# A packed-attention and feed-forward kernel: one table orders all engines up to the first rest, three quarters of one batch come first, and its second softmax has the tokens on the partitions

## The chip, the cores and the metric

The kernel runs on one core of one Trainium2 chip. The metric is the device time of one execution in microseconds. A core has the matrix engine TensorE (PE in the profile, PEld for its weight loads), VectorE (DVE), ScalarE (ACT), GpSimd (POOL) and SyncE (SP, which here only issues DMA transfers). Each works through its own queue in order and waits for the others by semaphores. SBUF is the working memory, PSUM (8 banks) takes what PE writes.

## The reference

`q`, `k`, `v` are [8, 8, 576, 64] (batch, head, token, width) and `p` is [8, 8, 32, 64], 32 "packs" for each head.

```python
def sm_attn(qq, kk, vv):
    s = scale * np.matmul(qq, kk.transpose(0, 1, 3, 2))
    s = s - np.max(s, axis=-1, keepdims=True)
    a = np.exp(s)
    a = a / (np.sum(a, axis=-1, keepdims=True) + 1e-09)
    return np.matmul(a, vv)
p_packed = sm_attn(p, k, v)                 # softmax over 576 tokens
out = sm_attn(q, p_packed, p_packed)        # softmax over 32 packs
x = out.transpose(0, 2, 1, 3).reshape(B * S, H * D)   # 4608 x 512
h = x @ w_in                                # 512 x 2048
return (h * sigmoid(h)) @ w_out             # 2048 x 512
```

## The kernel before

**Batches and units.** The feed-forward part never forms `out`. For each batch the packed result is multiplied into w_in (`packs_in`, a quarter of the 2048 columns at a time), and the second softmax's shares are the moving side of the hidden product. A unit (b, f) is 128 of the 2048 hidden columns of one batch. Its hidden product `h_unit` (L535) has 12 matmuls of 288 tokens, 6 for each half of the tokens, with upper and lower parts (`a_hi`, `a_lo`, `pw_hi`, `pw_lo`) for precision. ScalarE then makes `g` and `g_hi` (L538, L539), VectorE `g_lo` (L541), and the output product `out_unit` (L549) has 12 matmuls of 512 that add into PSUM over all f. Of the 288 tokens of a half, 256 go this way; the last 32 are collected in `rest` and come as four rest units for two batches.

**Attention of a batch.** First scores (L223, packs against keys), their maxima, an exponential, the exponentials turned so that tokens lie on the partitions, the packed product with `v` (L300), scaling, a turning of the result (L319), second scores (L223, packs against `q`). Then VectorE turns the second scores in 32x32 blocks (L336) so that each group of 32 packs lies along a row, takes maxima, subtracts (L339, L340), ScalarE exponentiates (L343), VectorE sums, divides and turns back (L346 to L353), and `a_hi` and `a_lo` are split (L357, L358).

**Weights.** `w_in` and `w_out` come as 64-bit numbers, 16 chunks of 1 MB, two in each quarter and matrix. Each is scaled by ScalarE (L172, L173), joined by VectorE (L178, L179, L181, and L182 for w_in; for w_out GpSimd adds, L182), and w_out is split (L190, L191).

**Order before.** Up to the mark where `manual_schedule` begins, a scheduler that plans with its own model of time puts the instructions in order, within pins (`PINS`, `WARM`, `STEPS`). The 32 early units run in `BLOCKS`, pairs (batch, quarter): two batches are interleaved, and each is added up in two parts (`parts` in DRAM). `keep_warm` (L107) multiplies the identity by itself. From the first rest on, the order is the program's, and batches 2 to 7 follow one another.

Of the kernel before, what the change touches and what calls it, by code (L numbers as in the profile page):

```python
# [19 lines left out]
P = 128  # L20
# [8 lines left out]
NJ = 4  # L29
# [8 lines left out]
BLOCKS = [(0, 0), (0, 1), (1, 0), (1, 1), (1, 2), (0, 2), (0, 3), (1, 3)]  # L38

WARM = (16, 2), (7, 4), (3, 2), (4, 2), (3, 2)  # L40
WARM_END = 10

PINS = (
    ("", "nm"),
    (("tT", 1), ("less", 0)),
    (("exp", 0), ("a2T", 0)),
    (("exp", 0), ("a2", 0)),
)

# [16 lines left out]
def packed_attention_ffn(ctx: ExitStack, tc: tile.TileContext, pkT, qT, vA, vB, w_in, w_out, out):  # L66

# [20 lines left out]
    ps_h = ent(tc.tile_pool(name="ps_h", bufs=1, space=PSUM))  # L88
    ps_s = ent(tc.tile_pool(name="ps_s", bufs=1, space=PSUM))
# [3 lines left out]
    win = const.tile([P, NJ, NI, JW], I32, name="win")  # L93
# [8 lines left out]
    def keep_warm(times):  # L102

        ps = ps_h.tile([P, 2, 512], F32, name="ps_hid")
        with after("pe"):
            for _ in range(times):
                made["pe"] = nc.tensor.matmul(ps[:, 0, :P], ident, ident, start=True, stop=True)  # L107

    def after(name):
        return tc.issue_after(made[name].ins) if name in made else nullcontext()  # L110

    def load_pk(b):
# [4 lines left out]
        return t[:, :P], t[:, P : P + NI * S].rearrange("p (hf i s) -> p hf i s", hf=2, i=NI)  # L117

    def load_q(b):
        t = kvq.tile([P, 5 * DM], F32, name="kvq_t")  # L120
        n = NI * HS
        for c in (slice(0, n), slice(n, 2 * n)) if b == 0 else (slice(0, 2 * n),):
            made["q_load", b] = nc.sync.dma_start(t[:, c], qT[b, :, c])
            if b == 0 and c.start == 0:
                weights.fetch(1)
        return t[:, : NI * S].rearrange("p (hf i s) -> p hf i s", hf=2, i=NI)

    def load_v(b):
        t = kvq.tile([P, 5 * DM], F32, name="kvq_t")
        nc.sync.dma_start(t[:, : 4 * DM], vA[b])  # L130
        nc.sync.dma_start(t[: S - 4 * P, 4 * DM :], vB[b])
        return t.rearrange("p (c e) -> p c e", c=5)

    class Weights:
# [5 lines left out]
        chunks = [(j, i, inner) for j in range(NJ) for inner in (True, False) for i in (0, 2)]  # L140

        def __init__(self, stage):
            self.stage, self.raw, self.n, self.fetched = stage, {}, 0, 0

            rings = [["stage", "stage", NJ - 2, NJ - 1], ["stage", "stage", NJ - 1], ["stage", "stage"]]
            self.place, self.after = [], []
            for n in range(len(self.chunks)):
                first = (0, 8, 12)[(n >= 8) + (n >= 12)]
                ring = rings[(n >= 8) + (n >= 12)]
                place = ring[(n - first) % len(ring)]  # L150
                before = [m for m in range(n) if self.place[m] == place]
                self.after.append((before[-2:-1] if place == "stage" else before[-1:]) or [-3])
                self.place.append(place)

        def fetch(self, ready):

            n = self.fetched
            if n == len(self.chunks) or self.after[n][0] > ready:
                return False
            self.fetched += 1  # L160
            if self.place[n] == "stage":
                raw = self.stage.tile([P, 4 * JW], I32, name="w_raw")
            else:
                raw = win[:, self.place[n]].rearrange("p i n -> p (i n)")
            j, i, inner = self.chunks[n]
            made["fetch", n] = nc.sync.dma_start(raw.bitcast(I64), (w_in if inner else w_out)[:, j, i // 2])
            self.raw[n] = raw.rearrange("p (n two) -> p two n", two=2)
            return True

        def scale(self, n):  # L170
            low, up = self.raw[n][:, 0], self.raw[n][:, 1].bitcast(F32)
            nc.scalar.activation(low, low.bitcast(U32), AF.Copy, scale=2.0**-29)  # L172
            nc.scalar.activation(up, up, AF.Copy, scale=2.0**-112)  # L173

        def join(self, n):
            j, i, inner = self.chunks[n]
            low, up = self.raw[n][:, 0], self.raw[n][:, 1]
            nc.vector.tensor_scalar(up.bitcast(F32), up.bitcast(F32), TOP, -TOP, op0=ALU.min, op1=ALU.max)  # L178
            nc.vector.scalar_tensor_tensor(low, up, -(2**31), low, op0=ALU.bitwise_and, op1=ALU.bitwise_or)  # L179
            z = win[:, j, i : i + 2].rearrange("p i n -> p (i n)") if inner else up  # L180
# [3 lines left out]
        def split(self, n):  # L184
            j, i, inner = self.chunks[n]
            w = self.raw.pop(n)[:, 1].bitcast(F32)
            if not inner:
                f = FJ * j + i
                hi, lo = (t[:, f : f + 2].rearrange("p i n -> p (i n)") for t in (wo_hi, wo_lo))
                nc.scalar.copy(hi, w)  # L190
                nc.vector.tensor_tensor(lo, w, hi.bitcast(F32), ALU.subtract)  # L191

        def step(self):

            n, last = self.n, len(self.chunks)
            self.n += 1
            while self.fetch(n - 2):
                pass
            if n < last:
                self.scale(n)  # L200
            if n - 1 in self.raw:
                self.join(n - 1)
                self.split(n - 1)

    def side_banks(b):

        if b:
            return ps_s.tile([P, 2, 512], F32, name="ps_side")
        return ps_acc.tile([P, 2, 512], F32, name="ps_acc")

    turns = [ps_h, ps_s]

    def two_banks():

        turns.reverse()
        return turns[0].tile([P, 2, 512], F32, name="ps_hid" if turns[0] is ps_h else "ps_side")

    def heads(bank, lhs, rhs, n):

        for par in range(2):  # L220
            r = slice(D * par, D * par + D)
            for i in range(NI):
                made["pe"] = nc.tensor.matmul(  # L223
                    bank(par)[NP * i : NP * i + NP, :n], lhs(r, i), rhs(r, i), start=True, stop=True
                )
# [4 lines left out]
    def attention(b):  # L230

        (p, k), v = made.pop(("kv", b))
        ps = [side_banks(b) for _ in range(2)] if b == 0 else []
        s1 = None if b == 0 else scratch(S).rearrange("p (r s) -> p r s", r=2)
        for hf in range(2):
# [496 lines left out]
```

## Time and profile before

| | us |
|---|---|
| three runs, median (lowest, highest) | 743.69 (743.69, 744.9) |
| profiled execution, time | 743.93 |
| profiled execution, span of its instructions | 742.1 |

Rows of a group read: line, engine, operation, output <- input, shapes, count, then busy time and mean ns of one, then the idle time of the engine just before them and what ended it. Rows of a timeline read: start, duration, engine, line, operation. A wait reads: who waited for whom, us in total, times, longest. A row of windows gives for each engine its busy time and count, then the granted TensorE clock, the DMA share and GB/s.

### The profile page before, as it was taken

To read this page: it belongs to the slowest core of one execution; us is meant where nothing else is said; L and a number is where in the kernel's file an instruction comes from. 1 tells how busy PE (TensorE), PEld (TensorE's weight loads), DVE (VectorE), ACT (ScalarE), POOL (GpSimd) and SP (SyncE) were. 2 spreads that over 40 slices of the span, in tenths; PEclk is the share of its full clock that TensorE was granted. 3 is DMA by queue.
4 is the path that set the end of the run, shared out by engine and by line. 5 is a ranking of instruction groups with operands and counts; after the bars stand their busy time and mean duration, and the time that the engine had idled before them with its cause. 6 is when DMAs were issued, how large, how long until landed. Compare 5 with 4: busy or idle time off the path is not lost.

```text
span 742.1 us, 11983 instructions
## 1 busy us (share of the span) xinstructions
PE 710.4 (96%) x5052; PEld 573.0 (77%) x5052; DVE 332.7 (45%) x487; ACT 330.6 (45%) x593; POOL 16.7 (2%) x14
## 2 busy tenths in 40 slices
PE   7659799999999999999999999999999999999997
PEld 6347577787777888788878888887888888787886
DVE  3975765565754233633362333633353233622111
ACT  4475656654643433535163442535163351533221
POOL 0011101101000000000000000000000000000000
PEclk9779999999999999999999999999999999999999
DMA  9854331334131213031301213031301210010001
GB/s 351 315 181 178 118 116 57 121 116 180 64 113 57 79 34 132 1 121 32 133 1 57 79 33 132 1 121 28 108 29 57 79 33 1 1 58 1 1 1 71
DMA packets 25813, 62.97 MB, mean 85 GB/s; under 512 B 14240, under 2 KB 14240, under 8 KB 20896
## 3 DMA queue, kind: packets, MB, share of 16 engines
q1 hardware_dynamic: 25664, 62.07, 23.9%
q8 instruction: 40, 0.66, 0.4%
q10 hardware_dynamic: 96, 0.13, 0.1%
q14 instruction: 13, 0.11, 0.0%
HBM read 47.71 MB, written 11.53 MB: 80 GB/s over the span
## 4 chain that ended last, share of the span: by engine, by line
PE 89%; DVE 5%; ACT 4%; DMA 1%; issue 1%; SPq 0%; ACTq 0%
PE ps_acc L549 53%; PE ps_hid L535 17%; PE ps_side L535 10%; PE ps_side L223 4%; PE ps_hid L223 2%; PE ps_hid L420 1%; DMA w_raw<-in_w_in 1%; DVE win L179 1%; PE ps_side L300 1%; ACT L538 1%; ACT g L538 0%; DVE pw_lo L500 0%; ACT g_hi L539 0%; ACT w_raw L172 0%; ACT w_raw L173 0%
## 5 line engine op out<-in xcount | busy, mean ns | idle before, releaser
L549 PE MATMUL ps_acc<-wo_hi,g_hi 128*128 128x512 f32 x576 | 232.8, 404 | 6.9 <-ACT g_hi L539 6.4
L549 PE MATMUL ps_acc<-wo_lo,g_hi 128*128 128x512 f32 x576 | 227.6, 396 | 0.0
L549 PE MATMUL ps_acc<-wo_hi,g_lo 128*128 128x512 f32 x576 | 223.5, 396 | 0.0
L541 DVE TENSOR_TENSOR g_lo<-g,g_hi 128x512 fp32r<-128x512 f32 x128 | 89.5, 699 | 289.8 <-ACT g_hi L539 289.8
L549 PEld LDWEIGHTS ps_acc<-wo_hi,g_hi 128*128 128x128 f32 x576 | 108.6, 189 | 51.4 <-issue 17.8
L549 PEld LDWEIGHTS ps_acc<-wo_hi,g_lo 128*128 128x128 f32 x576 | 108.8, 189 | 26.2 <-issue 0.8
L538 ACT ACTIVATE g<-ps_hid 128x512 f32<-128x512 f32 x80 | 48.0, 599 | 174.5 <-PE ps_hid L535 162.6
L549 PEld LDWEIGHTS ps_acc<-wo_lo,g_hi 128*128 128x128 f32 x576 | 108.7, 189 | 19.7
L535 PE MATMUL ps_hid<-a_hi,pw_hi 128*128 128x288 f32 x320 | 96.6, 302 | 6.2 <-ACT a_hi L357 4.1
L535 PE MATMUL ps_hid<-a_lo,pw_hi 128*128 128x288 f32 x320 | 95.9, 300 | 2.1 <-DVE a_lo L358 2.1
L535 PE MATMUL ps_hid<-a_hi,pw_lo 128*128 128x288 f32 x320 | 95.6, 299 | 0.0
L538 ACT ACTIVATE g<-ps_side 128x512 f32<-128x512 f32 x48 | 28.7, 599 | 127.7 <-PE ps_side L535 122.7
L535 PEld LDWEIGHTS ps_hid<-a_hi,pw_hi 128*128 128x128 f32 x320 | 61.2, 191 | 12.4 <-ACT a_hi L357 4.6
L535 PEld LDWEIGHTS ps_hid<-a_lo,pw_hi 128*128 128x128 f32 x320 | 61.3, 192 | 4.9 <-DVE a_lo L358 2.3
L535 PEld LDWEIGHTS ps_hid<-a_hi,pw_lo 128*128 128x128 f32 x320 | 61.5, 192 | 0.0
L535 PE MATMUL ps_side<-a_lo,pw_hi 128*128 128x288 f32 x192 | 56.6, 295 | 0.0
L535 PE MATMUL ps_side<-a_hi,pw_hi 128*128 128x288 f32 x192 | 56.6, 295 | 0.0
L535 PE MATMUL ps_side<-a_hi,pw_lo 128*128 128x288 f32 x192 | 56.5, 294 | 0.0
L539 ACT ACTIVATE g_hi<-ps_hid 128x512 fp32r<-128x512 f32 x80 | 47.4, 592 | 0.0
L535 PEld LDWEIGHTS ps_side<-a_hi,pw_hi 128*128 128x128 f32 x192 | 36.1, 188 | 1.8
L535 PEld LDWEIGHTS ps_side<-a_lo,pw_hi 128*128 128x128 f32 x192 | 36.1, 188 | 1.8
L535 PEld LDWEIGHTS ps_side<-a_hi,pw_lo 128*128 128x128 f32 x192 | 36.1, 188 | 0.0
(141 smaller groups left out, 661.0 us busy)
## 6 DMA issues: line engine op xcount, KB each, us to landing
kvq_t<-in_pkT SPq DMA_DIRECT2D x7, 1216.0 KB, 5.5
w_raw<-in_w_in SPq DMA_DIRECT2D x8, 1024.0 KB, 6.1
kvq_t<-in_vA SPq DMA_DIRECT2D x8, 1024.0 KB, 5.2
out<-o SPq DMA_DIRECT2D x16, 512.0 KB, 2.7
kvq_t<-in_qT SPq DMA_DIRECT2D x7, 1152.0 KB, 5.1
win<-in_w_out SPq DMA_DIRECT2D x5, 1024.0 KB, 7.4
w_raw<-in_w_out SPq DMA_DIRECT2D x3, 1024.0 KB, 4.7
parts<-o SPq DMA_DIRECT2D x4, 512.0 KB, 5.4
```

The costliest lines, as they stand in the source:

```text
L179: nc.vector.scalar_tensor_tensor(low, up, -(2**31), low, op0=ALU.bitwise_and, op1=ALU.bitwise_or)
L223: made["pe"] = nc.tensor.matmul(bank(par)[NP * i : NP * i + NP, :n], lhs(r, i), rhs(r, i), start=True, stop=True)
L300: made["pe"] = nc.tensor.matmul(psp[NP * i : NP * i + NP, par * D : par * D + D], e1T[:n, par, c, NP * i : NP * i + NP], v[:n, c, h * D : ...
L420: nc.tensor.matmul(bank[NP * i : NP * i + NP, par * D : par * D + D], self.e1T[:n, c, i, NP * par : NP * par + NP], self.v[:n, c, h * D : ...
L535: nc.tensor.matmul(ps[:, hf, :HS], p[:, par, cols], a[:, par], start=(n == 0), stop=(n == len(todo) - 1))
L538: silu = nc.scalar.activation(g.rearrange("p (h s) -> p h s", h=2), main, AF.Silu)
L539: nc.scalar.activation(g_hi.rearrange("p (h s) -> p h s", h=2), main, AF.Silu)
L541: lo = nc.vector.tensor_tensor(g_lo, g, g_hi.bitcast(F32), ALU.subtract)
L549: nc.tensor.matmul(bank, g[:, rows], w[:, f], start=(first and n == 0), stop=(last and n == 2))
```

## The change

From the start to the first rest, `manual_schedule` now covers PE, DVE, ACT and SP, and the steps run in the order of one table, `ORDER`. A step is a letter with numbers: `wf`, `ws`, `wz`, `wj`, `wu`, `wl` fetch, scale, clamp and sign, join and split a chunk; `a..` are steps of an attention (`aS0.1`: second scores of batch 0, second half); `p..` are pack products; `h`, `g`, `l`, `o` are a unit's hidden product, its ScalarE and VectorE part and its output product (`h0.1`: only the second half of the tokens); `W14` is 14 warm-up matmuls. Further:

- The blocks are quarters 0, 1, 2 of batch 0, all of batch 1, quarter 3 of batch 0, so that only batch 0 has its sums stored and loaded.
- The first quarter's weights come in eight chunks of half the size, and hidden columns 0 to 3 have pack products of their own. `w_in` lies by column blocks of 128.
- Batch 0's second softmax (`ON_TOKENS`): the queries are the stationary side, so the scores come with 128 tokens on the partitions; PE turns the shares back (`back2`).
- Batches 1 and 2 turn their first shares as later batches do, on VectorE with 16 small DMAs.
- The first four units run by halves. From the first rest on, the order is as before.

```diff
-BLOCKS = [(0, 0), (0, 1), (1, 0), (1, 1), (1, 2), (0, 2), (0, 3), (1, 3)]
+BLOCKS = [(0, 0), (0, 1), (0, 2), (1, 0), (1, 1), (1, 2), (1, 3), (0, 3)]
+PACKS = [(0, f, 1) for f in range(FJ)] + [(b, j * FJ, FJ) for b, j in BLOCKS[1:] + [(EARLY, 0)]]
+FIRST = [(0, True), (0, False), (1, True), (1, False), (2, True), (2, False), (3, True), (3, False)]
+CHUNKS = [(f, 1, inner) for f, inner in FIRST]
+CHUNKS += [(j * FJ + f, 2, inner) for j in range(1, NJ) for inner in (True, False) for f in (0, 2)]
+PLACES = ["new", "last", "new", "last", 8, 10, 12, 14]
+PLACES += ["new", "new", 8, 12, "new", "new", 12, "new", "new", "new", "new", "new"]
+ORDER = """
+wf0 ws0 wz0 k0 wf1 W2 wj0 as0.0 as0.1 wf2 ws1 am0.0 W14 ax0.0 am0.1 wf3 wz1 at0.0 v0 wj1 ax0.1 ay0.0 ws3 ws2
...
+"""
+ON_TOKENS = (0,)
-    win = const.tile([P, NJ, NI, JW], I32, name="win")
+    win = const.tile([P, NF, NI, P], I32, name="win")
...
+        def scores2(self, hf):
+            q = made["q", self.b]
+            ps = two_banks() if self.b else sum_banks()
+            self.half[hf] = ps
+            if self.b in ON_TOKENS:
+                blocks = [(ps, hf, P * c, P) for c in range(MAIN // P)]
+                if hf == 0:
+                    blocks += [(ps[REST * n : REST * n + REST], n % 2, MAIN, REST) for n in range(P // REST)]
+                for bank, part, s, n in blocks:
+                    for i in range(NI):
+                        for par in range(2):
+                            r = slice(D * par, D * par + D)
+                            at = slice(s + NP * i, s + NP * i + NP)
+                            lhs, rhs = q[r, part, i, s : s + n], made["packs", self.b](r, i)
+                            nc.tensor.matmul(bank[:, par, at], lhs, rhs, start=True, stop=True)
+                return
...
+        def back2(self, hf):
+            ps = self.back[hf] = two_banks() if self.b else sum_banks()
+            left = slice(REST * hf, REST * hf + REST)
+            for par in range(2):
+                for c in range(MAIN // P):
+                    at = slice(P * c, P * c + P)
+                    nc.tensor.transpose(ps[:, par, at], self.half[hf][1][:, par, at], ident)
+                some = self.half[0][1][left, par, MAIN:]
+                nc.tensor.transpose(ps[:, par, MAIN:HS], some, ident[left, left])
...
+            if self.b in ON_TOKENS:
+                self.half[hf] = self.half[hf], scratch(3 * P).rearrange("p (r s) -> p r s", r=2)
+                ps, t = self.on_tokens(hf)
+                mx, each = self.of_groups(ps)
+                nc.vector.tensor_reduce(mx, ps, axis=AX.X, op=ALU.max)
+                nc.vector.tensor_tensor(t, ps, each, ALU.subtract)
+                return
...
+    ent(tc.manual_schedule(engines={E.PE, E.DVE, E.Activation, E.SP}))
...
+    for step in ORDER.split():
+        which = step.rstrip("0123456789.")
+        steps[which](*map(int, step[len(which) :].split(".")))
```

The order of the built programs at three places. First PE's queue from its start in the kernel before: warm-up on `ident`, first scores into `ps_acc`, the turning of the exponentials `tm`, the packed product, the turning of `pp`, second scores with `ppT`.

```order
L107 MATMUL ps_hid<-ident 128x128 x16
L223 MATMUL ps_acc<-kvq_t 32x288 x16
L107 MATMUL ps_hid<-ident 128x128 x7
L275 MATMUL ps_acc<-ident,tm 128x128 x4
L276 MATMUL ps_acc<-ident,tm 64x128
L275 MATMUL ps_acc<-ident,tm 128x128 x4
L276 MATMUL ps_acc<-ident,tm 64x128
L300 MATMUL ps_acc<-kvq_t,tm 32x64 x40
L107 MATMUL ps_hid<-ident 128x128 x3
L319 MATMUL ps_acc<-ident,pp 128x128
L107 MATMUL ps_hid<-ident 128x128 x4
L223 MATMUL ps_acc<-kvq_t,ppT 32x288 x8
```

The same place in the changed kernel, from the first scores to the second; `ps_two<-win,ppT` are the first two small pack products.

```order
L211 MATMUL ps_acc<-kvq_t 32x288 x16
L132 MATMUL ps_two<-ident 128x128 x14
L276 MATMUL ps_acc<-ident,tm 128x128 x4
L276 MATMUL ps_acc<-ident,tm 64x128
L276 MATMUL ps_acc<-ident,tm 128x128 x4
L276 MATMUL ps_acc<-ident,tm 64x128
L132 MATMUL ps_two<-ident 128x128 x12
L309 MATMUL ps_acc<-kvq_t,tm 32x64 x40
L132 MATMUL ps_two<-ident 128x128 x5
L328 MATMUL ps_acc<-ident,pp 128x128
L211 MATMUL ps_two<-win,ppT 32x128 x16
L350 MATMUL ps_acc<-ppT,kvq_t 128x32 x16
```

The warm-up has moved from ahead of the first scores to behind them and between the later steps, and the second scores have the queries as weights (128x32 instead of 32x288).

Second, VectorE from the turned packs `ppT` on, in the kernel before: the blocks' turning, maxima and differences, with the second chunk of weights (`w_raw`, `win`) between them.

```order
L321 COPY ppT<-ps_acc 128x128
L336 STREAM_TRANSPOSE tm<-ps_acc 128x288 x2
L339 TENSOR_REDUCE mx_257<-tm 128x18
L340 TENSOR_TENSOR tm<-tm,mx_257 128x576
L178 TENSOR_SCALAR w_raw<-w_raw 128x1024
L336 STREAM_TRANSPOSE tm<-ps_acc 128x288 x2
L179 SCALAR_TENSOR_TENSOR w_raw<-w_raw 128x1024
L181 TENSOR_SCALAR win<-w_raw 128x1024
L346 TENSOR_REDUCE sm<-tm 128x18
L339 TENSOR_REDUCE mx_287<-tm 128x18
```

In the changed kernel, from the lower parts of the small pack products on:

```order
L460 TENSOR_TENSOR pw_lo<-ps_two,pw_hi 128x2x128 x2
L387 TENSOR_REDUCE on_tokens<-ps_acc 128x24
L388 TENSOR_TENSOR tm<-ps_acc,on_tokens 128x768
L460 TENSOR_TENSOR pw_lo<-ps_two,pw_hi 128x2x128
L387 TENSOR_REDUCE on_tokens<-ps_acc 128x16
L388 TENSOR_TENSOR tm<-ps_acc,on_tokens 128x2x256
L408 TENSOR_REDUCE on_tokens<-tm 128x24
L409 TENSOR_SCALAR on_tokens<-on_tokens 128x24
L410 RECIPROCAL on_tokens<-on_tokens 128x24
L411 TENSOR_TENSOR tm<-tm,on_tokens 128x768
```

The block transposes are gone, maxima are taken from PSUM, and no weights stand between the steps of the softmax here.

Third, VectorE from the first `a_lo` to the second, in the kernel before:

```order
L358 TENSOR_TENSOR a_lo<-tm,a_hi 128x576
L178 TENSOR_SCALAR win<-win 128x1024
L181 TENSOR_SCALAR win<-win 128x1024
L349 TENSOR_TENSOR tm<-tm,sm 128x576
L179 SCALAR_TENSOR_TENSOR win<-win 128x1024
L353 STREAM_TRANSPOSE tm<-tm 128x576
L181 TENSOR_SCALAR win<-win 128x1024
L244 COPY tm<-ps_side 128x2x288
L358 TENSOR_TENSOR a_lo<-tm,a_hi 128x576
```

And in the changed kernel:

```order
L433 TENSOR_TENSOR a_lo<-ps_acc,a_hi 128x576
L184 TENSOR_SCALAR w_raw<-w_raw 128x1024
L185 SCALAR_TENSOR_TENSOR w_raw<-w_raw 128x1024
L184 TENSOR_SCALAR win<-win 128x512
L185 SCALAR_TENSOR_TENSOR win<-win 128x512
L433 TENSOR_TENSOR a_lo<-ps_acc,a_hi 128x576
```

Fewer and partly smaller pieces of weights stand between the two, and the second half's shares are ready ahead of the first `a_lo`.

More of the change, by code (lines that the diff above doesn't have):

```diff
@@ L100, in packed_attention_ffn, with two_banks, sum_banks, keep_warm @@
     made = {}
[L102 to L112, printed above, removed]
+    def two_banks():
+        return ps_two.tile([P, 2, 512], F32, name="ps_two")
+    def sum_banks():
+        return ps_acc.tile([P, 2, 512], F32, name="ps_acc")
+    def keep_warm(n):
+        ps = two_banks()
+        for _ in range(n):
+            nc.tensor.matmul(ps[:, 0, :P], ident, ident, start=True, stop=True)
+    def load_k(b):
         t = kvq.tile([P, 5 * DM], F32, name="kvq_t")
@@ L155, in fetch @@
[L155 to L162, printed above, removed]
-            else:
[L164 to L168, printed above, removed]
+            self.stage, self.raw = stage, {}
@@ L213, in two_banks, with both, upper, lower @@
[L213 to L218, printed above, removed]
+        def both(self, n):
+            f, nf, _ = CHUNKS[n]
+            return (t[:, f : f + nf].rearrange("p i n -> p (i n)") for t in (wo_hi, wo_lo))
+        def upper(self, n):
+            hi, _ = self.both(n)
+            nc.scalar.copy(hi, self.raw[n][1].bitcast(F32))
+        def lower(self, n):
+            hi, lo = self.both(n)
+            nc.vector.tensor_tensor(lo, self.raw[n][1].bitcast(F32), hi.bitcast(F32), ALU.subtract)
@@ L595, in load_parts @@
             outs["o", b, h] = o
+    E = mybir.EngineType
+    ent(tc.manual_schedule(engines={E.PE, E.DVE, E.Activation, E.SP}))
     scope = ExitStack()
     weights = Weights(scope.enter_context(tc.tile_pool(name="stage", bufs=2)))
-    k0 = load_pk(0)
-    weights.fetch(0)
-    made["kv", 0] = k0, load_v(0)
-    first = attention(0)
-    for warm, slices in WARM:
-        keep_warm(warm)
-        with after("pe"):
-            for _ in range(slices):
-                next(first, None)
-    with after(("q_load", 0)):
-        while weights.fetch(-1):
-            pass
@@ L650, in packed_attention_ffn @@
-    for _ in ahead:
-        pass
-    E = mybir.EngineType
-    ent(tc.manual_schedule(engines={E.PE, E.DVE, E.Activation, E.SP}))
+    attention = [Attention(b) for b in range(B)]
+    packs = [Packs(*which) for which in PACKS]
+    steps = {
+        "W": keep_warm,
+        "k": load_k,
+        "v": load_v,
+        "q": load_q,
+        "wf": weights.fetch,
+        "ws": weights.scale,
+        "wz": weights.sign,
+        "wj": weights.join,
+        "wu": weights.upper,
+        "wl": weights.lower,
+        "h": h_products,
+        "g": h_values,
+        "l": h_lower,
+        "o": out_products,
+        "e": out_rows,
+        "b": load_parts,
+    }
@@ new lines, in packed_attention_ffn @@
+    names = dict(s="scores1", c="copied1", m="largest1", x="exps1", r="shares1", t="turned1", y="spread1", a="packed")
+    names |= dict(n="scaled1", i="turned", j="packs", S="scores2", T="turned2", M="less2", X="exps2", D="shares2")
+    names |= dict(H="upper2", L="lower2", U="back2")
+    for letter, name in names.items():
+        steps["a" + letter] = lambda b, *args, name=name: getattr(attention[b], name)(*args)
+    for letter, name in dict(p="products", u="upper", l="lower").items():
+        steps["p" + letter] = lambda n, name=name: getattr(packs[n], name)()
@@ L687, in packed_attention_ffn @@
         if step:
-            getattr(coming, step)()
-        out_unit(u)
+            step_of(b + 1, step)
+        out_products(u)
+        if f == NF - 1:
+            for h in range(2):
+                out_rows(u, h)
         if step == "packed":
-            coming.packs()
+            attention[b + 1].turned()
+            attention[b + 1].packs()
 def _laid_out(q, k, v, p, moe_w_in, moe_w_out):
```

737 lines of the change are left out of this document (331 added, 406 removed).

## The prediction

> **What bounds the kernel now.** I read the page first: the busy shares and the slices over the span.
>
> ```profile
> PE 710.4 (96%) x5052; PEld 573.0 (77%) x5052; DVE 332.7 (45%) x487; ACT 330.6 (45%) x593; POOL 16.7 (2%) x14
> PE   7659799999999999999999999999999999999997
> DVE  3975765565754233633362333633353233622111
> PEclk9779999999999999999999999999999999999999
> ```
>
> TensorE (PE) is full in every slice but the first six (18.55 us each) and the last. In those first slices VectorE (DVE) is the busier engine, and the granted TensorE clock sinks to 0.7. All that can be won lies there. Next I cut the span by windows, at two marks of the program: 34.39 us, the first product of the hidden layer, and 233.07 us, where the first product of batch 2 begins.
>
> ```profile
> core 0: us, PE busy (x) PEld busy (x) DVE busy (x) ACT busy (x) POOL busy (x), PEclk, DMA share, GB/s
> 34.39:110.00 75.61, 59.52 (x437) 45.13 (x430) 53.70 (x71) 48.16 (x68) 8.45 (x4) 0.91 0.42 146
> 110.00:233.07 123.07, 121.48 (x821) 93.58 (x819) 72.95 (x94) 67.32 (x110) 7.57 (x4) 1.00 0.30 107
> 233.07:742.10 509.03, 504.78 (x3534) 416.00 (x3532) 184.31 (x284) 200.09 (x396) 0.00 (x0) 1.00 0.16 52
> ```
>
> From 233.07 us the order of instructions on every engine is the same in both kernels, so those 509.03 us stay. The question is when the changed kernel reaches that mark. What the first 233 us must hold I count in PE work at full pace, from pieces of the chain of waits in the undisturbed part (start, us, what) and two rows of PE's timeline:
>
> ```profile
> 237.60 1.59 PE ps_hid L535 x12
> 239.19 2.77 PE ps_acc L549 x12
> 276.75 1.66 PE ps_hid L420 x80
> 445.64 1.66 PE ps_hid L420 x80
> ```
>
> ```profile
> 7.49 1.20 PE L223 MATMUL ps_acc<-kvq_t 64*32 64x288 f32 x32
> 223.80 1.09 PE L223 MATMUL ps_hid<-win,ppT 64*32 64x512 f32 x16
> ```
>
> A unit is one hidden product (1.59) and one output product (2.79 with its gap), 4.38 us. Other pieces: packed attention (80 instructions) 1.66, a pair of score halves 1.13 and a quarter of the packs through w_in 1.02 (the last two rows less the 0.07 that the next instruction overlaps), the turning of the packs 0.27. Two batches then need 32 x 4.38 + 4 x 2.79 + 2 x (1.13 + 1.66 + 0.27 + 1.13 + 4 x 1.02) = 168 us, and the two L420 rows, two batches apart, lie 168.9 us apart: the count holds. From 34.39 to 233.07 the kernel before has 32 units, two rest units (5.6), two attentions with their transposes on PE (11.6) and ten pack quarters (10.2): **167.6 us of work in 198.7 us**. Of the 31.1 us lost, 16.1 + 1.6 are idle by the windows above; the clock of 0.91 costs some 5.4 (9% of 59.5); 8 are thin stretches that no row shows as idle. PE's waits name who ends them:
>
> ```profile
> PE ps_acc L549 <- ACT g_hi L539: 6.4, 4, 2.9
> PE ps_side L223 <- DVE win L182: 5.2, 1, 5.2
> PE ps_hid L535 <- ACT a_hi L357: 4.1, 1, 4.1
> PE ps_hid L535 <- DVE a_lo L358: 2.1, 1, 2.1
> ```
>
> These are weights being joined and the first batch's shares, both through VectorE.
>
> **The change, step by step: the way to the first product.** PE's own rows in the kernel before (start, us, instructions):
>
> ```profile
> 8.62 1.83 PE L107 MATMUL ps_hid<-ident 128*128 128x128 f32 x14
> 12.02 0.66 PE L275 MATMUL ps_acc<-ident,tm 128*128 128x128 f32 x4 [1.57 <-ACT tm L262]
> 14.77 1.73 PE L300 MATMUL ps_acc<-kvq_t,tm 128*32 128x64 f32 x80 [1.27 <-DVE tm L279]
> 18.51 0.71 PE L223 MATMUL ps_acc<-kvq_t,ppT 64*32 64x288 f32 x16
> 40.20 0.40 PE L535 MATMUL ps_hid<-a_hi,pw_hi 128*128 128x288 f32 x1 [4.09 <-ACT a_hi L357]
> 42.66 0.61 PE L535 MATMUL ps_hid<-a_lo,pw_hi 128*128 128x288 f32 x1 [2.06 <-DVE a_lo L358]
> ```
>
> A warm-up matmul is two instructions of 0.13 (1.83 over 14). Fewer stand ahead of the scores now (2 matmuls, not 16), but I leave the scores ending at 8.6, because they must run on a clock that nothing warmed. After them stand 14 matmuls (28 x 0.13 = 3.6): the turning of e1 starts at 12.3, not 12.02. Twelve more (3.1) stand between it and the packed product, which starts at 16.8 instead of 14.77, and five, not three, after that (+0.5). So the packs are turned at 20.3, two small pack products (a quarter of 1.02 and a gap, 0.3 each) follow, and the second scores begin at **20.9 instead of 18.51**.
>
> **Second scores with tokens on the partitions.** Before: 2 x 16 instructions, 0.72 us each half. Now 48 matmuls in the first half and 16 in the second, two instructions each: 96 and 32. No row shows a 32-column matmul with 128-column weights. Lower end: the L300 row, 1.73 over 80, 0.022 each: 2.8 us in all. Upper end: a warm-up instruction, 0.13: 16.7. I take 0.08 for the 64 instructions with 128-column weights (their weights are those of the warm-up, their moving side a quarter) and 0.05 for the 64 with 32-column weights (nearest L300, but eight in a row share one column group): 5.8 + 2.6 = **8.4**. The Trainium skill, page "TensorEngine Tiling (Array Packing)", section Instruction Overhead, says that a matmul pays about 60 cycles however few its columns are. By that 128 instructions come to an estimated 3.2 us and the end 5 us earlier; the L300 row is near it, but there four lie side by side.
>
> What goes in exchange are VectorE's transposes: two of the scores and one of the shares per half. The costs that I use, from the groups of the first 240 us:
>
> ```profile
> L541 DVE TENSOR_TENSOR g_lo<-g,g_hi 128x512 fp32r<-128x512 f32 x33 | 24.0, 726 | 53.2 <-ACT g_hi L539 53.2
> L179 DVE SCALAR_TENSOR_TENSOR w_raw<-w_raw 128x1024 int32<-128x1024 int32 x11 | 13.4, 1220 | 0.2
> L182 DVE CUSTOM_DVE_ANT_0 win<-w_raw,win 128x2048 uint16<-128x2048 uint16 x8 | 9.8, 1221 | 0.2
> L178 DVE TENSOR_SCALAR w_raw<-w_raw 128x1024 f32<-128x1024 f32 x11 | 7.6, 692 | 2.4 <-ACT w_raw L173 2.4
> L349 DVE TENSOR_TENSOR tm<-tm,sm 128x576 f32<-128x576 f32 x6 | 4.5, 756 | 0.2
> L172 ACT ACTIVATE w_raw<-w_raw 128x1024 int32<-128x1024 uint32 x11 | 13.1, 1193 | 8.3 <-DMA w_raw<-in_w_in 7.9 <-DMA w_raw<-in_w_out 0.4
> L343 ACT ACTIVATE tm<-tm 128x576 f32<-128x576 f32 x6 | 4.1, 686 | 7.7 <-DVE tm L340 7.7
> ```
>
> Scores end at 26.7 and 29.3; pack product 2 and its copy, which now stand ahead of the first exponential on PE and ScalarE, end at 29.9; the exponential of 768 (0.69 for 576, so 0.85) at 30.7. VectorE takes the second half's maxima to 31.4, the first half's shares (two passes over 768 of 0.95, from 0.756 at 576, small ones 0.3) to 33.6, the second half's to 35.1 (its exponential came behind two 512-wide scalings, each two ACTIVATEs of half of 1.19). Turned back by PE (6 x 0.16) each half is in PSUM by 36.0. On VectorE one sign step (0.9) and the first a_lo (0.7) give 36.8; two sign steps (1.7 and 0.9) and the second a_lo give **40.1**. The first hidden product so starts at 36.8 (34.39 before), and the second half's lower part comes at 40.1 (42.66 before): 2.6 won.
>
> **From there to unit 8: VectorE.** Three quarters of batch 0 first means that w_in and w_out of quarters 0 to 2 must be joined by unit 8, where the kernel before needs quarter 2 at unit 16. Between the second a_lo and the turning of batch 1's first shares, just ahead of hidden product 10, VectorE now has 76 instructions: 15 TENSOR_SCALAR x 0.69, 7 of L179's kind and 4 of L182's x 1.22, 5 subtractions of 1024 x 1.22, 6 g_lo x 0.69, 17 half-size ones (about 0.43 or 0.69, from 1.22 at 1024 and 0.69 at 512): 42.4; attention of batch 1: 12.5. That is 54.9 us, and successive ones overlap by 0.09 each, so **48.0**:
>
> ```profile
> 12.01 1.23 DVE L179 SCALAR_TENSOR_TENSOR w_raw<-w_raw 128x1024 int32<-128x1024 int32 x1
> 13.15 0.68 DVE L181 TENSOR_SCALAR win<-w_raw 128x1024 int32<-128x1024 int32 x1
> ```
>
> The second starts 1.14 after the first, which lasts 1.23. GpSimd's additions lengthen some:
>
> ```profile
> 35.34 2.33 POOL L182 TENSOR_TENSOR win<-win 128x1024 int32<-128x1024 int32 x1 [34.04 <-DVE win L181]
> 35.84 2.91 DVE L179 SCALAR_TENSOR_TENSOR win<-win 128x1024 int32<-128x1024 int32 x1
> ```
>
> 2.91 instead of 1.22 beside one addition; four full and two half-size ones fall in the stretch, and I add 3. PE has 48.8 us to do there (10 hidden and 9 output products, 4.2 of attention, 3.4 of packs), from 36.8: ready at 85.6 if never kept waiting. VectorE is later: 40.1 + 48.0 + 3 = **91.1**.
>
> Of the moved DMAs, batch 1's turned shares now go through 16 transfers on SP's queue. They took 10.44 us to issue and 1.9 to land in later batches:
>
> ```profile
> 263.07 10.44 SPq L411 DMA_DIRECT2D tm<-tm  x16
> ```
>
> VectorE ends its transposes near 52, they land near 64, and VectorE comes to scale the packed result near 70. That hides them by 6 us; if SP's queue is held up by more than that, the end moves with it.
>
> **The remainder.** All PE work from the first hidden product to the mark: 32 units 140.2, rest 5.6, attentions 8.4 (3.2 less, the transposes are VectorE's and the DMA's), packs 10.5, warm-up 0.3: 165.0. Less 48.8 leaves 116.2, in which VectorE's share is as low as in the second window. The saved and reloaded partial sums fall from four halves to two; they stood beside PE work (1.6 idle in 123) and I give nothing for them. I add 4 for thin stretches, half of the 8 found before; later batches show nearly none. Mark: 91.1 + 116.2 + 4 = **211.3 instead of 233.07, 21.8 us earlier**. The profiled execution took 743.93 us (its span and 1.83 around it), so 722.2; the median of the runs shown is 0.24 lower: **722.0**.
>
> **The clock.** Warm-up falls from 43 matmuls to 34, and PE idles up to 4 us between 29.6 and 36.8.
>
> ```profile
> 40.00:50.00 10.00, 6.57 (x22) 5.72 (x23) 8.17 (x10) 8.20 (x11) 1.89 (x1) 0.52 0.36 130
> ```
>
> Here the clock was 0.52 and PE busy for 6.57, so about 3.2 us were lost. I give nothing, since VectorE sets the pace at that point. The Trainium skill, page "TensorE: Matmul & The Clock Gate", section on HAM oscillation, says that an idle gap beyond about 3.4 us halves the clock until activity lasts again. The row agrees. By that rule the cold stretch comes again, and the sum would be 725 if it were on the path.
>
> **The rivals.**
> - *VectorE's waits stay as scattered as before.* An order written out for all engines makes each wait for its own next step, even where another could run. Then the 48.8 us of PE work go at the rate of the first window (59.52 of 75.61 busy, at 0.91: 0.72), 68 us: 36.8 + 68 + 116.2 + 8 = 229, **740**. For it: VectorE is needed for 51 of 54 us. Against it: before, VectorE idled 21.9 us in that window, so work was at hand in the wrong order.
> - *Exposed weight loads make the token scores slow.* Each of the 128 instructions brings its own weights. These are the warm-up's rows (ns: min/median/max):
>
> ```profile
> L107 PEld LDWEIGHTS ps_hid<-ident x86: 186/272/338, 1.4 to 33.2; 128*128 128x128 f32 x86
> L107 PE MATMUL ps_hid<-ident x86: 274/377/582, 1.4 to 33.4; 128*128 128x128 f32 x86
> ```
>
>   If none is hidden, 128 x 0.272 = 34.8 instead of 8.4, straight in the chain: 26.4 later, **749**, slower. The point of no gain is (8.4 + 21.8) / 128 = 0.236 us each. Against it: warm-up instructions follow each other in 0.13 although each load lasts 0.186 or more.
> - *PE runs dense at once.* With token scores at their lower end (-5.6), no lengthening by GpSimd (-3) and no thin stretches (-4): **710**.
>
> **How the numbers follow.** Forecast's own range: 710 to 734 (token scores at the upper end add 8.3, thin stretches 4 more), chance 0.72. Below 710: 0.03. Scattered waits, 734 to 742: 0.13. No change: 0.04. Slower: 0.08. 710 to 738 leaves out the 0.03 below and, above it, 0.05 of the scattered waits, no change and slower: together 0.2. About 0.2% (1.5 us) is what a measurement of this kernel can tell from no change.
>
> **What would show it.** Right: second scores starting near 21 and lasting 6 and 3 us; the first hidden product near 37; VectorE nearly gapless from there to about 90; unit 8's output near 91; PE idle under 3 us after that; batch 2 beginning near 211; the last 509 us unchanged. Wrong: token scores over 17 us; VectorE idle for over 10 us between 40 and 90; PE waiting for a transfer of batch 1's shares or of weights; a clock of 0.5 after 50; or any change after the mark.

## The result, and the profile after

| | before | after |
|---|---|---|
| median (lowest to highest), us | 743.69 (743.24 to 744.9) | 714.54 (713.68 to 715.36) |
| profiled execution, span, us | 742.1 | 711.9 |

The ratio is 0.9605 (95% interval 0.9589 to 0.9622), 29.2 us less. The page of the changed kernel shows, for the rows that the prediction began with, busy shares and the 40 slices (17.8 us each now):

```profile
PE 695.0 (98%) x5170; PEld 570.4 (80%) x5170; DVE 332.7 (47%) x504; ACT 325.0 (46%) x612; POOL 18.7 (3%) x16
PE   7699999999999999999999999999999999999997
DVE  5899986535543336332562325533362334622112
PEclk9789999999999999999999999999999999999999
```

PE is full from the third slice on; before, it was from the sixth. VectorE's slices three to five are full as well (36 to 89 us). The windows of the changed kernel, cut where its first hidden product begins (36.17), where unit 8's output product ends (90.59) and where batch 2's first product begins (207.48):

```profile
core 0: us, PE busy (x) PEld busy (x) DVE busy (x) ACT busy (x) POOL busy (x), PEclk, DMA share, GB/s
36.17:90.59 54.42, 52.92 (x431) 41.20 (x424) 53.19 (x76) 42.69 (x76) 9.87 (x6) 0.96 0.59 213
90.59:207.48 116.89, 116.85 (x822) 94.72 (x821) 69.57 (x96) 62.57 (x108) 5.91 (x3) 1.00 0.29 100
207.48:711.90 504.42, 500.14 (x3534) 415.74 (x3532) 184.34 (x284) 200.12 (x396) 0.00 (x0) 1.00 0.16 52
```

In the first of them PE is busy for all but 1.5 us and VectorE for all but 1.2; in the second PE idles 0.04. The longest of PE's waits in the changed kernel (who waited for whom, us, times, longest):

```profile
PE ps_acc L378 <- DVE tm L411: 4.8, 1, 4.8
PE ps_acc L211 <- DMA kvq_t<-in_pkT: 3.9, 2, 3.7
PE ps_two L132 <- POOL ident masks.py:199: 1.4, 1, 1.4
PE ps_two L309 <- DMA tm<-tm: 1.3, 1, 1.3
```

The four waits for weights and shares that the prediction quoted (17.8 us) are gone; the turning back of batch 0's shares waits 4.8 in their place, and batch 1's turned shares come 1.3 late by their 16 transfers. The 3.9 stand ahead of the first scores, where the kernel before ran its first 16 warm-up matmuls, and the 1.4 for the identity were there before. Batch 2's first product comes 25.6 us earlier (207.48, not 233.07). But the last row above is 504.42 long, not 509.03, though no instruction in it stands in another place. The chain of waits has packed attention two batches apart as the prediction used it (start, us, what), in the changed kernel:

```profile
250.87 1.66 PE ps_two L309 x80
418.29 1.66 PE ps_two L309 x80
```

167.42 us, where the kernel before takes 168.89. So 4.6 of the 30.2 us come from a stretch that the change doesn't touch.

### The profile page after: what moved, and what is told of

Read it like the earlier page. It is cut to its first block, busy times and chain, and to the rows that moved or that the text cites. A ratio compares the mean times of both kernels' runs of the same rounds, so it can differ in the third digit from the quotient of the medians.

```text
span 711.9 us, 12319 instructions
## 1 busy us (share of the span) xinstructions
PE 695.0 (98%) x5170; PEld 570.4 (80%) x5170; DVE 332.7 (47%) x504; ACT 325.0 (46%) x612; POOL 18.7 (3%) x16
## 4 chain that ended last, share of the span: by engine, by line
PE 94%; DVE 2%; SPq 1%; DMA 1%; issue 0%; ACT 0%; ACTq 0%
PE ps_acc L520 55%; PE ps_two L488 28%; PE ps_two L211 7%; PE ps_two L309 2%; SPq L288 1%; PE ps_two L132 1%; DMA kvq_t<-in_pkT 1%; PE ps_acc L350 1%; PE ps_acc L378 0%; DMA tm<-tm 0%; DVE g_lo L513 0%; PE ps_acc L309 0%; DVE tm L270 0%; DVE mx L247 0%; DVE w_raw L185 0%
## 5 line engine op out<-in xcount | busy, mean ns | idle before, releaser
L513 DVE TENSOR_TENSOR g_lo<-g,g_hi 128x512 fp32r<-128x512 f32 (+1 forms) x132 | 90.9, 688 | 263.8 <-ACT g_hi L507 263.8
L506 ACT ACTIVATE g<-ps_two 128x512 f32<-128x512 f32 (+1 forms) x132 | 77.5, 587 | 275.8 <-PE ps_two L488 258.7
L488 PE MATMUL ps_two<-a_hi,pw_hi 128*128 128x288 f32 x512 | 153.2, 299 | 0.1
L488 PE MATMUL ps_two<-a_lo,pw_hi 128*128 128x288 f32 x512 | 152.0, 297 | 0.0
L488 PE MATMUL ps_two<-a_hi,pw_lo 128*128 128x288 f32 x512 | 151.2, 295 | 0.0
L520 PEld LDWEIGHTS ps_acc<-wo_hi,g_hi 128*128 128x128 f32 x576 | 108.0, 188 | 40.6 <-issue 21.0
L488 PEld LDWEIGHTS ps_two<-a_hi,pw_hi 128*128 128x128 f32 x512 | 96.9, 189 | 8.5 <-ACT rest L508 1.4
L488 PEld LDWEIGHTS ps_two<-a_lo,pw_hi 128*128 128x128 f32 x512 | 96.7, 189 | 3.6
L488 PEld LDWEIGHTS ps_two<-a_hi,pw_lo 128*128 128x128 f32 x512 | 96.7, 189 | 0.0
L507 ACT ACTIVATE g_hi<-ps_two 128x512 fp32r<-128x512 f32 (+1 forms) x132 | 76.6, 580 | 6.3 <-PE ps_acc L520 6.3
L460 DVE TENSOR_TENSOR pw_lo<-ps_two,pw_hi 128x1024 fp32r<-128x1024 f32 (+1 forms) x35 | 38.3, 1126 | 13.9 <-ACT pw_hi L457 13.9
L508 ACT ACTIVATE rest<-ps_two 128x64 f32<-128x64 f32 (+1 forms) x132 | 30.2, 229 | 0.0
```

What stands on the lines that cost most here:

```text
L460: nc.vector.tensor_tensor(self.lo, self.ps[:, :, : self.nf * P], self.hi.bitcast(F32), ALU.subtract)
L488: nc.tensor.matmul(bank, p[:, par, cols], a[:, par], start=(n == 0), stop=(n == len(todo) - 1))
L506: nc.scalar.activation(g, ps[..., :MAIN], AF.Silu)
L507: nc.scalar.activation(g_hi, ps[..., :MAIN], AF.Silu)
L508: nc.scalar.activation(to, ps[..., MAIN:HS], AF.Silu)
L513: nc.vector.tensor_tensor(g_lo[:, c], g[:, c], g_hi[:, c].bitcast(F32), ALU.subtract)
```

## The experiments

All but the last were timed in three rounds beside the kernel before, the last in five. The changed kernel was not timed again with them, and its own executions lie 1.7 us apart. So a difference of some 1.5 us or less from its 714.54 isn't told from none by the times; there the profiles have to speak, one execution of each kernel.

**Where the quicker tail comes from.** In the changed kernel the groups of the tail (260 to 660 us) show one difference, the output product; first before, then after (count, busy us, mean ns):

```profile
L549 PE MATMUL ps_acc<-wo_lo,g_hi 128*128 128x512 f32 x338 | 133.4, 395 | 0.0
```

```profile
L520 PE MATMUL ps_acc<-wo_lo,g_hi 128*128 128x512 f32 x343 | 134.2, 391 | 0.0
```

The hidden products are alike (295 and 296). The small tiles `on_tokens` move `g`, `g_hi` and `g_lo` from address 191744 to 192128 in each partition; `wo_hi` and `wo_lo` stay. Four kernels move tiles alone (g and the pools that lie behind it; in e9 all but the identity). e1 and e2, a tile that nothing uses ahead of the pool of g, 96 floats in the kernel before and 160 in the changed one:

```diff
+    pad = ent(tc.tile_pool(name="pad", bufs=1)).tile([P, 96], F32, name="pad")
     gp = ent(tc.tile_pool(name="gp", bufs=2))
```

> The kernel before with 384 unused bytes ahead of the g tiles, so that g, g_hi and g_lo lie at the addresses that they have in the changed kernel (192128 and on instead of 191744); no instruction differs. In the changed kernel the matmuls of an output product follow each other in 0.229 us, in the kernel before in 0.232, all through the run. Theory A, the place of the g tiles decides that step: 1728 x 0.0035 = 6 us less, 737 to 738 us, step 0.229. Theory B, something else in the changed program does: 743.7 as before, step 0.232.

> The changed kernel with 640 unused bytes ahead of the g tiles (192768, which is the place of before plus 1024). Theory A, the place of the g tiles decides the step of the output product: 720 to 721 us and a step of 0.232. Theory B: 714.5 and 0.229.

e8 has the same line in the changed kernel; e9 has 32 floats ahead of `win`:

> The changed kernel with 384 unused bytes ahead of the g tiles, which then lie at 192512, a multiple of 1024. So far the output product's step was 0.232 with them at 256 past a multiple of 1024 (two kernels) and 0.229 at 640 past it (four kernels; wo_hi and wo_lo also lie at 640 past one). If a boundary that a row of weights crosses costs the time: 0.229 or less, 713 to 714.5. If it is the same place within 1024 as wo's that helps: 0.232, 720.5.

> The changed kernel with 128 unused bytes ahead of win, so that all tiles but ident move by 128: wo_hi and wo_lo from 640 past a multiple of 1024 to 768, g_hi and g_lo from 640 to 768 as well. The step of the output product was 0.229 us where g and wo stand at the same place within 1024, 0.232 where they don't. If the relation of the two decides: 0.229, 714.5. If the place of g by itself does (640 quick; 0 and 256 slow): 0.232, 720 to 721.

| kernel | g_hi past a multiple of 1024 | wo_hi | mean ns of that group | time, us |
|---|---|---|---|---|
| before | 256 | 640 | 395 | 743.69 |
| e1, before, g moved | 640 | 640 | 391 | 738.0 |
| after | 640 | 640 | 391 | 714.54 |
| e2, after, g moved | 256 | 640 | 395 | 720.34 |
| e8, after, g moved | 0 | 640 | 395 | 721.65 |
| e9, after, all moved | 768 | 768 | 391 | 714.54 |

The row of e1 in the same window, with no instruction of the kernel before changed (its lines are one higher):

```profile
L550 PE MATMUL ps_acc<-wo_lo,g_hi 128*128 128x512 f32 x342 | 133.8, 391 | 0.0
```

And that of e2:

```profile
L521 PE MATMUL ps_acc<-wo_lo,g_hi 128*128 128x512 f32 x340 | 134.2, 395 | 0.0
```

From batch 2's first product to the end, e1 and then e2:

```profile
231.72:736.20 504.48, 500.20 (x3534) 415.76 (x3532) 184.39 (x284) 200.15 (x396) 0.00 (x0) 1.00 0.16 52
```

```profile
209.34:718.40 509.06, 504.82 (x3534) 415.96 (x3532) 184.37 (x284) 200.13 (x396) 0.00 (x0) 1.00 0.16 52
```

Theory A holds both ways: the kernel before gets the changed one's tail (504.4), and the other way round (509.0). The place of g is worth 5.7 us in the one kernel (7.3 against the 745.33 of the kernel before's runs beside e1; e1's ratio to them is 0.991, 0.988 to 0.994; by the spans, 742.1 and 736.2, 5.9) and 5.8 in the other. The changed kernel also has other PSUM pools in the tail (`ps_two` for `ps_hid` and `ps_side`). e1 keeps the old ones and is as quick, so they aren't the cause.

e9 refutes that 640 by itself is the quick place, and e8 that a multiple of 1024 is: quick is where the tiles of g and wo begin at the same place within 1024 bytes. But 1024 is not the step that counts. An output product takes g in four blocks of 128 tokens, three matmuls each, and these blocks lie 512 bytes apart, while wo's rows start 2048 apart. So in the quick kernels two blocks of four stand 512 off from wo within 1024. The first matmuls of the second, third and fourth block, and what follows them, in the changed kernel:

```profile
272.11 0.39 PE L520 MATMUL ps_acc<-wo_hi,g_hi 128*128 128x512 f32 x1
...
272.79 0.39 PE L520 MATMUL ps_acc<-wo_hi,g_hi 128*128 128x512 f32 x1
...
273.47 0.39 PE L520 MATMUL ps_acc<-wo_hi,g_hi 128*128 128x512 f32 x1
...
274.15 0.29 PE L488 MATMUL ps_two<-a_hi,pw_hi 128*128 128x288 f32 x1
```

Each block takes 0.68, the second and fourth no more than the third. So it is the place within 512 or within 256 bytes: by 512 the distances tried are 0, 128 and 384, by 256 they are 0 and 128, and by 128 all would be the same.

**What the order is worth.** e5 has the same steps and blocks, but the planning scheduler orders them up to the first rest:

```diff
-    ent(tc.manual_schedule(engines={E.PE, E.DVE, E.Activation, E.SP}))
     scope = ExitStack()
...
+    ent(tc.manual_schedule(engines={E.PE, E.DVE, E.Activation, E.SP}))
     scope.close()
```

> The changed kernel with the same steps written in the same sequence, but the four engines' order up to the first rest left to the planning scheduler (the manual order begins at the first rest, as in the kernel before). Blocks, half-size chunks, softmax on the tokens and the g tiles' addresses stay. Theory order (most of the 25.6 us ahead of batch 2 come from the table's hold over the queues, the work itself is nearly the same): 728 to 738. Theory work (they come from the blocks, the softmax and the smaller chunks, whoever orders them): 715 to 720.

It took 755.17, ratio to before 1.0152 (1.0135 to 1.0169): more than theory "order" foresaw. PE's waits in it:

```profile
PE ps_acc L378 <- DVE tm L411: 18.8, 1, 18.8
PE ps_acc L520 <- ACT g_hi L507: 8.1, 7, 2.7
PE ps_two L488 <- DVE a_lo L433: 2.9, 1, 2.9
```

The planner puts weights ahead of the first shares on VectorE (18.8 us of wait for 4.8). So the change's work without its order is 11.6 us slower than the kernel before, and 40.6 slower than with it. In the profiles the first hidden product comes 19.5 us later than in the changed kernel (55.67), batch 2's first product 41.9 later (249.35), and the tail is the same (504.45). The kernel before had pins for its planner and this one has none, so e5 shows what the steps are worth without the table, and not what the best order of a planner would give. The blocks and the half-size chunks were not undone one by one, nor was the kernel before's work put under a table: what they add is open.

**The second softmax on the tokens.** e3 undoes it:

```diff
-ON_TOKENS = (0,)
+ON_TOKENS = ()
```

In the table `aT0.0` and `aT0.1` stand for `aU0.0` and `aU0.1`, behind the scores.

> The changed kernel with batch 0's second softmax by block transposes as in the kernel before (one step aT for each half, no turning back on PE); unused bytes keep the g tiles at the changed kernel's addresses. VectorE has 2.7 us more to do there (10.1 instead of 7.5), PE about 5 us less (scores 1.4 instead of 4.75, no back2). Theory VectorE (it sets the pace until the first unit of batch 1): the second a_lo 1 to 2 us later, 715.5 to 716.5. Theory scores (the chain through the 4.75 us of scores sets the first hidden product): 2 to 3 earlier, 711.5 to 712.5.

It took 716.36, 1.8 more (2.1 by the spans): theory VectorE. PE's timeline shows how the chain differs from the changed kernel's:

```profile
32.45 0.61 PE L489 MATMUL ps_two<-a_hi,pw_hi 128*128 128x288 f32 x1 [1.10 <-ACT a_hi L430]
36.21 0.61 PE L489 MATMUL ps_two<-a_lo,pw_hi 128*128 128x288 f32 x1 [3.15 <-DVE a_lo L434]
...
39.81 0.61 PE L489 MATMUL ps_two<-a_lo,pw_hi 128*128 128x288 f32 x1 [0.21 <-DVE a_lo L434]
```

The first product starts 3.7 us earlier there, and it helps nothing: the lower parts come with VectorE, the second half's at 39.8 instead of 38.5. That is 1.2 of the 2.1. In e3 the first six matmuls of the output product also run at half clock (2.37 us, 1.38 in the changed kernel), which is about the rest.

**Half clock and half units.** e4 fills PE's wait for the first shares with warm-up, e11 runs units 0 to 3 whole:

```diff
-ws5 aD0.0 aX0.1 aU0.0 wf9 aD0.1
+ws5 aD0.0 aX0.1 W18 aU0.0 wf9 aD0.1
```

> The changed kernel with 18 more warm-up matmuls in the 4.8 us in which PE waits for the first shares (26.7 to 31.5). Clock theory (the first hidden products at 0.24 instead of 0.133 are on the path): the first 24 products and the transposes of the shares 2.5 to 3.5 us shorter, 711.5 to 713. VectorE theory (PE is waited for by nobody there): 714.5, within 0.5.

> The changed kernel with units 0 to 3 whole, not by halves of the tokens: hidden product 0 waits for the second a_lo (38.5 instead of 36.2), VectorE's eight half subtractions become four (0.6 us less), ScalarE's 24 small activations become 12. Theory PE (dense behind its first hidden product): 1.2 to 1.7 us of half-clock work of unit 0 come later, less some 0.5 for fewer starts of small groups, 715.2 to 716.2. Theory VectorE: 0.6 less work, 713.9 to 714.5.

e4 took 715.51, outside both ranges. Its first 15 hidden matmuls run at full clock, and PE then waits where it didn't:

```profile
PE ps_two L488 <- ACT rest L508: 1.3, 1, 1.3
...
PE ps_two L488 <- DVE tm L237: 0.4, 1, 0.4
```

The windows show that the half clock only moved:

```profile
33.35:41.41 8.06, 6.09 (x61) 3.79 (x60) 7.80 (x14) 7.05 (x13) 1.48 (x2) 1.00 0.28 95
41.41:44.58 3.17, 3.17 (x12) 2.60 (x11) 3.10 (x6) 2.58 (x9) 0.85 (x1) 0.52 0.42 165
```

The first six matmuls of the output product now take 2.56 us, not 1.38. So e4 neither confirms nor refutes the clock theory: what the clock is worth stays open. Besides, the 18 were too many (the first shares' turning back starts at 33.35, and their last step had ended at 32.1), and the token scores took 5.82 in its profile instead of 4.75. e11 took 714.35, in the range of theory VectorE and no difference that the times can tell: the halves neither win nor cost.

**Who sets the pace from 36 to 91 us.** e6 gives VectorE more to do, behind eight g_lo steps (`d0`); e7 takes a wait out of its queue; e12 is e7 with less for it:

```diff
+    def more_work(n):
+        nc.vector.tensor_tensor(pad, pad, pad, ALU.subtract)
```

> The changed kernel with eight more subtractions of 128x512 on VectorE (about 0.6 us each in a row, 4.8 in all, on a tile that nothing uses), one behind each of the g_lo steps l1.0 to l6, that is between 46 and 82 us; the g tiles' addresses move by 2048 bytes. Theory VectorE sets the pace until unit 12: only 1.6 us of wait (at 102) and 0.4 us ahead of the first product of batch 1 take some of it up, so 2.8 to 4.8 us more, 717.3 to 719.3. Theory PE sets the pace and VectorE runs ahead of it: 714.5, within 0.7.

```diff
-aM0.0 wf8 pp2 pu2 aX0.0 pl2 ws7 aM0.1 k1 ws5 aD0.0 aX0.1 aU0.0
+aM0.0 wf8 aX0.0 pp2 pu2 ws7 aM0.1 pl2 k1 aX0.1 ws5 aD0.0 aU0.0
```

> The changed kernel with both exponentials of batch 0's second softmax moved ahead of other work in ScalarE's queue: the first stands ahead of the upper part of pack product 2 (which waits for all scores), the second ahead of a chunk's scaling; pack product 2's lower part stands behind the second half's maxima on VectorE. The first shares come 1.5 to 1.9 us earlier and VectorE loses its wait of 1.77 us. Theory VectorE (its queue from there to unit 12 has no room): the end moves with it, 712.6 to 713.2. Theory PE (its products from 42 us on bound): 714.5, within 0.5. The other side: weights then join later, PE waits for them at the first output products, 715 to 716.

```diff
+            if not inner:
+                nc.vector.scalar_tensor_tensor(up, up, 3, low, op0=ALU.logical_shift_left, op1=ALU.bitwise_or)
+                return
...
-            (nc.vector if inner else nc.gpsimd).tensor_tensor(z, z, low, ALU.add)
+            nc.vector.tensor_tensor(z, z, low, ALU.add)
```

> The kernel of e7_exp_first with w_out's chunks joined by one VectorE instruction (shift left by 3, then bitwise or) in place of a shift on VectorE and an addition on GpSimd; left out is the carry of an addition whose lower part rounds up to 8. From 38 to 94 us VectorE so has 0.5 us more for each of four full chunks and 0.3 for each of two half ones (2.7), and loses the 3.6 us by which its instructions were lengthened beside GpSimd's additions (2.38 for 0.68, 1.53 for 0.69 and the like). Theory VectorE (queue full to unit 12, lengthening as read from the profile): 0.9 less there and some 0.2 before, 712.2 to 712.8. Theory PE (dense behind the first hidden product): 713.5, within 0.5. The other side, the lengthening was work that would be waited for anyway: 714.5 to 716.

e6 took 718.97, 4.4 more for 4.8 of work. The stretch from the first hidden product to unit 8's output in its profile:

```profile
36.92:95.67 58.75, 53.51 (x432) 40.17 (x424) 58.06 (x84) 42.52 (x76) 9.86 (x6) 0.99 0.57 197
```

58.75 us, not 54.42, and VectorE with hardly a gap. e7 took 713.48 (ratio 0.9588, 0.957 to 0.9606): its first product starts at 34.54, 1.63 earlier, and its span is 710.2, 1.7 less. That is the fastest with e12, but its interval overlaps that of the changed kernel, and the time lies between the two theories (712.6 to 713.2, 714.0 to 715.0). e12 took 713.44. The same stretch in e7 and then in e12:

```profile
34.54:88.95 54.41, 52.79 (x431) 40.44 (x424) 53.16 (x76) 42.58 (x76) 9.86 (x6) 0.97 0.60 213
```

```profile
34.46:88.77 54.31, 52.29 (x431) 40.24 (x424) 52.47 (x76) 42.69 (x76) 0.00 (x0) 0.98 0.61 213
```

VectorE has 0.7 less to do, and the stretch is 0.1 shorter: theory PE. More work for VectorE lengthens the stretch, 0.7 less doesn't shorten it, and an earlier start moves the whole of it. Two engines are at their limit together, as far as these two sizes tell. The end of the stretch goes with VectorE's second a_lo rather than with PE's first product: from the end of the second a_lo to the end of unit 8's output it is 52.1 us in the changed kernel and in e7, 52.0 in e12 and 52.2 in e11, although e11's first product starts 1.2 us later than the changed kernel's. In e3 and e4 it is 53.0 and 52.9; these are the two whose first output product ran at half clock.

**Fewer warm-ups.** e10 is e7 with `W8` for `W14`, `W7` for `W12`, and `ws2` behind `ay0.1`.

> The kernel of e7_exp_first with 8 warm-up matmuls for 14 and 7 for 12, and the second scaling of the two that stand ahead of ScalarE's copy of the turned exponentials moved behind it. In the profile of e7 the warm-up ends 1.9 us after the first exponential and the second one 1.8 us after both copies, so the chain to the first hidden product can come up to 3 earlier. Theory chain (PE is dense behind the first hidden product, so the end goes with it): 710.5 to 711.5. Theory VectorE (weights fill its queue from 14 us on, it can give 1.2 to 2 at most): 711.5 to 712.5. The other side: fewer warm-ups leave the clock at half for the scores (5.7 instead of 4.7 us in three profiles), 713.5 to 714.5.

It took 714.06, the "other side". The packed product started 1.46 earlier than in e7 (15.08, not 16.54); then PE's timeline has

```profile
19.11 0.33 PE L328 MATMUL ps_acc<-ident,pp 128*128 128x128 f32 x1 [0.99 <-DVE pp L319]
19.91 0.67 PE L211 MATMUL ps_two<-win,ppT 64*32 64x128 f32 x32 [0.47 <-DVE ppT L332]
20.51 6.84 PE L350 MATMUL ps_acc<-ppT,kvq_t 64*128 64x32 f32 x128
```

VectorE, busy with weights, scaled the packs no earlier, and the scores took 6.84 instead of 4.75. How much of this comes from the fewer warm-ups is open. e2, e4, e6, e8, e9 and e11 run the changed kernel's matmuls up to the scores, and theirs took 5.38, 5.82, 5.66, 5.0, 4.87 and 4.75: the length varies without any change to the warm-ups.

## Why the prediction was right, and where it wasn't

| step | predicted | measured |
|---|---|---|
| second scores begin | 20.9 | 20.62 |
| they last | 8.4 | 4.75 |
| first hidden product | 36.8 | 36.17 |
| second a_lo ends | 40.1 | 38.52 |
| unit 8's output ends | 91.1 | 90.59 |
| batch 2 begins | 211.3 | 207.48 |
| from there to the end | 509.03 | 504.42 |

The direction, the place and the mechanism were right: waits scattered over the first 90 us go, and e5 shows that the same steps without the table don't take them away. The time was forecast 7.5 us too long (722.0 against 714.54; by spans 720.3 against 711.9, 8.4). By the table 0.6 of the 8.4 lie ahead of the first product, nothing between it and unit 8 (54.3 forecast, 54.42 measured), 3.3 between unit 8 and batch 2, and 4.6 behind.

*The last 509 us stay* failed, by one of the signs that the prediction had named ("any change after the mark"). The argument was that the order on every engine is the same, and it is; the addresses are not. With g at its old place (e2) the changed kernel takes 720.34, and the forecast of 722.0 would be 1.7 off. The same quickening is about 1.0 of the 3.3 between unit 8 and batch 2 (25 output products there, 300 of the 1728 matmuls to which the 5.8 us belong).

*Four us of thin stretches* is the rest of the 3.3: 116.2 us of work were counted at the old place of g, 115.2 at the new one, and 116.89 were taken, so 1.7 of the 4 came.

*Second scores 8.4* was mis-sized, by 3.7. The row in the changed kernel, and the wait that followed:

```profile
20.62 4.75 PE L350 MATMUL ps_acc<-ppT,kvq_t 64*128 64x32 f32 x128
...
31.51 0.66 PE L378 MATMUL ps_acc<-ident,tm 128*128 128x128 f32 x2 [4.79 <-DVE tm L411]
```

0.037 each, between the L300 row's 0.022 and the warm-up's 0.13, and much nearer the lower end; I had chosen 0.08 and 0.05. The 60 cycles of the Trainium skill, page "TensorEngine Tiling (Array Packing)", section Instruction Overhead, gave an estimated 3.2, nearer than mine and still too low. Little of the 3.7 reached the first product: the first shares were ready 2.2 us earlier than forecast (31.4 against 33.6), and then the turning back and half of batch 1's scores ran on a half clock (3.51 and 1.15, from 31.51 to 36.17). So the 36.8 came nearly true by luck: the forecast had it wait for the first a_lo on VectorE, which was done at 34.92, and it waited for PE itself, on a half clock that the sum had put at nothing.

*VectorE sets the pace to unit 8* gave the right time for a reason that holds on one side only. The forecast had PE ready at 85.6 and VectorE at 91.1. VectorE is indeed busy 53.19 of 54.42 us, and more work for it costs nearly its whole length (e6). But PE needed 54.42 for what I counted as 48.8: 1.3 wait for the transfers, 2.3 half clock (36.17 to 40.70), some 2 the starts of small groups. So that both came out at the same time is partly luck, and taking 0.7 of VectorE's work away wins nothing (e12). The 3 us that I added for GpSimd's additions do lengthen VectorE's instructions (3.6 in the profile); whether they are a term of the path e12 can't say, because it put 2.7 us of other work in their place.

*The clock is worth nothing there* is open: in e4 the half clock only moved, and in e3 and e4, where it reached the first output product, unit 8 came 0.8 to 0.9 us later after the second a_lo. *16 transfers hidden by 6 us* failed, the other sign that the prediction had named: they landed near 64 as forecast, but the packed product came for them at 62 and waited 1.3 us, which is part of PE's 54.42.

The reading of the slices was too broad as well: VectorE is the busier engine only in the second and third of the first six, and PE is full from the sixth. No sum rests on it.

The rivals: scattered waits (740) did not come with the table, but came with the planner (e5, 755). Exposed weight loads (0.272 each) did not come, at 0.037. "PE runs dense at once" (710) was nearest in kind: from 40.7 on PE idles 1.5 us in 167, and 714.5 lies between it and the forecast.

## What to carry to other kernels

Before calling a stretch unchanged because its instructions are, compare the addresses of the tiles that stream through TensorE together: an unused tile of 384 bytes was worth 5.7 us of 744. Where two engines are both full, price work added to one at nearly full length (4.4 for 4.8 on VectorE here) and don't count on work taken from one (0.7 less won 0.1). And an order that keeps both fed is worth more here than the steps that were undone alone (1.8 for the second softmax, none for the halves): the same steps in the order of a planner without pins took 40.6 us longer.

## What the runs showed of the hardware

The output product (stationary g, 128x128; moving wo, 128x512) follows itself 3 to 4 ns later where g stands 128 or 384 bytes off wo's place within 512 than where both stand at the same. The hidden products (moving 288) don't differ between the kernels, but most of their tiles weren't moved, so this is no test of them. Why was not tried. The Trainium skill, page "SBUF — State Buffer", section "SBUF: two separate sides", names two points of contention, the port that GpSimd shares with VectorE and the ports of the DMA. The first it is not: GpSimd does nothing in the tail (0.00 busy). For the second there is no sign: the tail's DMA share is 0.16 in the quick kernels and in the slow ones.

The granted clock fell while PE was working. In e10, whose scores begin at 20.51 and leave no gap, the windows show:

```profile
20.51:22.00 1.49, 1.49 (x36) 1.49 (x28) 1.46 (x4) 0.60 (x2) 0.00 (x0) 1.00 1.06 423
22.00:24.00 2.00, 2.00 (x78) 1.89 (x76) 1.41 (x4) 0.00 (x0) 0.00 (x0) 0.60 1.03 426
24.00:26.00 2.00, 2.00 (x22) 2.00 (x22) 1.75 (x2) 0.12 (x1) 0.00 (x0) 0.50 1.02 422
```

1.00, then 0.60, then 0.50, with PE busy throughout; the longest wait of the 6 us ahead of them was 0.99. The same 128 matmuls took 4.75 in the changed kernel and in e7, 5.82 in e4, 6.84 in e10, and 8.48 in e5, where the clock was 0.50 from their start. The Trainium skill, page "TensorE: Matmul & The Clock Gate", section on HAM oscillation, has the clock fall by idle gaps over some 3.4 us; the wait of 4.79 above agrees with it (1.00 up to the wait, 0.50 behind it), this doesn't. Nor does the fall in e4 at 41.4, where the longest wait since 33.35 was 1.3. Matmuls of 64 rows and 32 columns may not be enough to hold the clock up, which is an inference from these profiles; in the changed kernel it stayed at 1.00 through all 128 of them.
